# A hand-planned attention and feed-forward kernel: new keys for the planner's order on TensorE and in the head

## The chip, the cores and the metric

The kernel runs on one core of a Trainium2 chip. The core has five engines with an instruction stream each: TensorE (PE in the profile; its weight loads are listed as PEld), VectorE (DVE), ScalarE (ACT), GpSimd (POOL) and SyncE (SP), which here issues all the DMA transfers. The metric is the device time of one execution in microseconds, lower is better.

## The reference

Sparse attention over 8 batches, 8 heads, 576 positions and 64 dimensions, then a feed-forward network (FFN) on the 4608 tokens:

```python
scores = scale * np.matmul(q, k.transpose(0, 1, 3, 2))
thresh = np.max(scores, axis=-1, keepdims=True) - tau
scores = np.where(scores >= thresh, scores, -1000000000.0)
scores = scores - np.max(scores, axis=-1, keepdims=True)
attn = np.exp(scores)
attn = attn / (np.sum(attn, axis=-1, keepdims=True) + 1e-09)
out = np.matmul(attn, v)
...
h = x @ w_in
g = np.where(h >= beta, h, np.where(h <= -beta, 0.0, (h + beta) ** 2 / (4.0 * beta)))
return g @ w_out
```

Here x is the attention's output with the heads side by side (512 columns), w_in is 512 x 2048, w_out 2048 x 512, and beta is 1. The two weights come as 64-bit floats.

## The kernel before

**The planner.** The kernel doesn't write its instructions in program order. It describes each piece of work as an operation of a `Plan` (L40): an engine, an estimated cost, a key, what it comes after, and the buffers that it takes and uses. `Plan.order` (L73) then plays the engines forward in time: whenever an engine is free, it gets, among the operations whose predecessors are done and whose buffers are free, the one with the lowest key. The resulting list is the order in which the instructions are put into each engine's stream, and on the chip every engine works through its stream in that order. A key is thus a priority in the order, counted in units of attention tiles; an operation that isn't ready is passed over, whatever its key. Some chains have a fixed order of their own (`behind`): score products among themselves, products with V, first FFN products, second FFN products.

**Attention.** All matmuls work on values split into two 16-bit parts. Each batch has four pairs of heads. For each pair q and k are loaded, squared and summed for a scale, normalized on POOL, split by ACT and POOL, and copied by DMA into the layout that the matmuls need (`add_qk`, L287). V is handled once per batch (`add_v`, L369). The queries are cut into parts (batch, pair, half): the first half has 256 queries, the second 320, and all four first halves of a batch come ahead of the second halves. A part is cut into 4 or 5 tiles of 128 rows, 36 tiles in a batch, 288 in all. `add_tile` (L603) does one tile j, and nearly all its operations have the key j: the scores (PE, into one of two slots `s` of two PSUM banks each), the maximum (DVE), the exponential (ACT), the mask with the sum (DVE), the normalization (POOL), the split (ACT and POOL), and a transposing DMA into `eT`. When the last tile of a part is done, `add_av` (L669) multiplies by V on PE into one of three banks `ph` and splits the result into the buffer `x` of a group of tokens; its key is that of the part's last tile plus one. There are five `x` buffers, two of which serve as staging space for w_out until it is loaded.

**Weights.** `add_w` (L424) loads each weight in 16 units, converts each on DVE from 64 bits (three operations), sums its squares on PE (`gram`), and, when the scale is known, normalizes and splits it (ACT, ACT, POOL). The units of w_in are staged in eight places, those of w_out in two. The key of unit u comes from a function; its load stands 5 below it. For a pair of q and k the loads stand 6 below its key, for V 8 below.

**FFN.** A group of 256 tokens is worked on in pieces of 128 tokens, each in four steps of 512 hidden columns: `ffn1` (48 matmuls into a bank `ph`), `relu` and `square` (ACT), `gate` (DVE), `ghi` (ACT) and `glo` (DVE) into one of four buffers `g`, and `ffn2` (12 matmuls into the only bank `acc`); there are 144 such steps. The key `kf` of a step starts at the group's last attention tile plus `LEAD`, or goes on from the step before, and rises by 2 with each step, so that the four steps of 128 tokens take 8 units, as many as there are tiles for 128 tokens. After the fourth step `acc` is scaled by ACT and stored.

The loop that sets the keys of the loads:

```python
for b in range(B):
    for p in range(NPAIR):
        t0 = start[b, p, 0]
        add_qk(b, p, t0 if (b, p) != (0, 0) else -20)
    add_v(b, start[b, 0, 0] + (0 if b else 4))
add_w("i", lambda u: 0.7 * u - 2)
add_w("o", lambda u: 10 + 0.5 * u)
```

For batch 0 `start` is 0, 4, 8 and 12 for the four pairs.

Of the kernel before, what the change touches and what calls it, by code (L numbers as in the profile page):

```python
# [17 lines left out]
P = 128  # L18
GN = 256
FW = 512  # L20
LEAD = 8
EXPM = 0x7F000000
ESC = 2.0 ** 15

# [127 lines left out]
def attn_ffn_kernel(ctx: ExitStack, tc: tile.TileContext, qT, kT, vT, tau, w_in, w_out, out):  # L152
# [14 lines left out]
    NVB = NEB + 5  # L167
# [6 lines left out]
    plan = Plan()  # L174
# [53 lines left out]
    def ap(b, arr):  # L228
        return arr[b.slot]
# [40 lines left out]
    for i, (b, p, h) in enumerate(parts):  # L270
        first[i] = len(tiles)
        n, q0 = (S1, S0) if h else (S0, 0)
# [8 lines left out]
    start = {x: first[i] for i, x in enumerate(parts)}  # L281
# [267 lines left out]
    for b in range(B):  # L549
        for p in range(NPAIR):  # L550
            t0 = start[b, p, 0]
            add_qk(b, p, t0 if (b, p) != (0, 0) else -20)
        add_v(b, start[b, 0, 0] + (0 if b else 4))
    add_w("i", lambda u: 0.7 * u - 2)
    add_w("o", lambda u: 10 + 0.5 * u)

# [15 lines left out]
    for b in range(B):  # L574
        s, wi, wo = scs[:, b, :], wsc["i"], wsc["o"]
# [19 lines left out]
    part_tr = {}  # L595
    eTb = {}
    prev = {}

    def chained(name, o):
        prev[name] = o  # L600
        return o

    def add_tile(j):  # L603
        i, v, heads, col = tiles[j]
        b, p, h = parts[i]
        cb, qb, kb, ready, c2 = QK[b, p]
        s, e, x, m = plan.buf("s"), plan.buf("e"), plan.buf("hl"), plan.buf("sm")
        if i not in eTb:
            eTb[i] = plan.buf("eT")
            part_tr[i] = []  # L610

        def qk():
            q, k = ap(qb, qq), ap(kb, kk)
            for f in range(2):
                for l in range(2):
                    for hd, c in heads:
                        r = slice(0, P) if len(heads) == 1 else slice(hd * D, (hd + 1) * D)
                        n = r.stop - r.start
                        T.matmul(ap(s, s_ps)[r, f, :SH], q[:, hd, c : c + n], k[:, hd, l, f * SH : (f + 1) * SH], start=l == 0, stop=l == 1)  # L619

        def sv():
            return ap(s, s_ps)[:, :, :SH]

        def halves(t):
            return t.rearrange("p (f n) -> p f n", f=2)

        def smax():

            t, c = ap(m, sm), ap(cb, pc)
            V.tensor_reduce(t[:, 0:1], sv(), AX.XY, ALU.max, negate=True)  # L630
            V.tensor_scalar(t[:, 1:2], t[:, 0:1], c[:, 24 + v, 0:1], None, ALU.mult)  # L631
            V.tensor_scalar(t[:, 2:3], t[:, 0:1], -1.0, c[:, 27 + v, 0:1], ALU.mult, ALU.add)

        def sexp():
            A.activation(halves(ap(e, es)), sv(), AF.Exp, bias=ap(m, sm)[:, 1:2], scale=ap(cb, pc)[:, 24 + v, 0:1])  # L635

        def smask():
            t = ap(m, sm)
            V.scalar_tensor_tensor(halves(ap(e, es)), sv(), t[:, 2:3], halves(ap(e, es)), ALU.is_ge, ALU.mult, accum_out=t[:, 3:4])  # L639

        def sden():
            t = ap(m, sm)
            V.tensor_scalar(t[:, 4:5], t[:, 3:4], 1e-9, 1.0 / ESC, ALU.add, ALU.mult)  # L643
            V.reciprocal(t[:, 5:6], t[:, 4:5])

        def snorm():
            G.tensor_scalar(ap(e, es), ap(e, es), ap(m, sm)[:, 5:6], 1.0, ALU.mult, ALU.mult)  # L647

        def shi():
            A.activation(ap(x, hl)[:, :S], ap(e, es), AF.Copy)  # L650

        def slo():
            G.tensor_tensor(ap(x, hl)[:, S:], ap(e, es), ap(x, hl)[:, :S], ALU.subtract)  # L653

        def send():
            Y.dma_start_transpose(ap(eTb[i], eT)[:, :, col : col + P], ap(x, hl))

        o = chained("qk", plan.op("PE", 0.5 if len(heads) == 1 else 0.7, j, qk, ready, take=[s], uses=[qb, kb], behind=prev.get("qk")))
        o = chained("max", plan.op("DVE", 0.95, j, smax, [o, c2], take=[m], uses=[s, cb], behind=prev.get("max")))
        o = chained("exp", plan.op("ACT", 0.73, j, sexp, [o], take=[e], uses=[s, m, cb], behind=prev.get("exp")))  # L660
        o = plan.op("DVE", 0.82, j, smask, [o], uses=[s, m, e])
        o = plan.op("DVE", 0.26, j, sden, [o], uses=[m])
        o = chained("norm", plan.op("POOL", 0.77, j, snorm, [o], uses=[e, m], behind=prev.get("norm")))
        o = chained("hi", plan.op("ACT", 0.58, j, shi, [o], take=[x], uses=[e], behind=prev.get("hi")))
        o = plan.op("POOL", 1.26, j, slo, [o], uses=[e, x])
        o = chained("tr", plan.op("SP", 1.3, j, send, [o], take=[eTb[i]] if j == first[i] else [], uses=[x, eTb[i]], work=1.7, behind=prev.get("tr")))
        part_tr[i].append(o)

    def add_av(i):  # L669
        b, p, h = parts[i]  # L670
        n = S1 if h else S0
        pb = plan.buf("ph")
        vbuf, vready = VV[b, p]
        cuts, takes, xu = [], [], []
        p0 = h * S0
        for g, pieces in enumerate(groups):
            for gb_, t0, c0, m in pieces:
                lo, hi = max(t0, p0), min(t0 + m, p0 + n)
                if gb_ != b or lo >= hi:
                    continue  # L680
                if not xdone[g]:
                    takes.append(xbuf[g])
                xu.append(xbuf[g])
                cuts.append((g, slice(lo - p0, hi - p0), slice(c0 + lo - t0, c0 + hi - t0)))

        def av():
            o = ap(pb, ph)
            t = ap(eTb[i], eT)
            vt = ap(vbuf, vst)
            for k in range(NVB):  # L690
                kb = k if k < NEB else k - NEB
                for hd in range(2):
                    T.matmul(o[hd * D : (hd + 1) * D, :n], vt[:, k, hd * D : (hd + 1) * D], t[:, kb, hd * n : (hd + 1) * n],  # L693
                             start=k == 0, stop=k == NVB - 1)

        def xpart(g, l, c):
            return ap(xbuf[g], xb).bitcast(F16).rearrange("p (c l n) -> p c l n", c=NCC, l=2)[:, p, l, c]

        def hi():
            for g, src, c in cuts:  # L700
                A.activation(xpart(g, 0, c), ap(pb, ph)[:, src], AF.Copy, scale=1.0 / ESC)

        def lo():
            for g, src, c in cuts:
                V.scalar_tensor_tensor(xpart(g, 1, c), ap(pb, ph)[:, src], 1.0 / ESC, xpart(g, 0, c), ALU.mult, ALU.subtract)  # L705

        key = last[i] + 1
        m = len(cuts)
        o = chained("av", plan.op("PE", NVB * n / 2400 + 0.2, key, av, part_tr[i] + [vready], take=[pb], uses=[eTb[i], vbuf], behind=prev.get("av")))
        o = chained("avhi", plan.op("ACT", n / 1200 + 0.06 * m, key, hi, [o], take=takes, uses=[pb] + xu, behind=prev.get("avhi")))  # L710
        o = plan.op("DVE", n / 960 + 0.06 * m, key, lo, [o], uses=[pb] + xu)
        for g, _, _ in cuts:
            xdone[g].append(o)
            xlast[g] = max(xlast[g], last[i])

    for j in range(NS):
        add_tile(j)
        i = tiles[j][0]
# [7 lines left out]
    kf, nstep = 0.0, 0  # L726
    n, k = P, FW // P
    for g, c0 in [(g, c0) for g in range(NG) for c0 in range(0, gtok[g], P)]:
        kf = max(kf, xlast[g] + LEAD)
        ab = plan.buf("acc")  # L730
        ends = []
        bs = [b for b, _ in segs(g)]
        for fc in range(0, NFC, k):
            hb, tb, qb = plan.buf("ph"), plan.buf("asq"), plan.buf("g")
# [52 lines left out]
            wo = [wlo["o", x] for x in range(fc, fc + k)]  # L787
# [4 lines left out]
            o = chained("f1", plan.op("PE", 48 * 0.056, kf, ffn1, xdone[g] + wi, take=[hb], uses=[xbuf[g]], behind=prev.get("f1")))  # L792
            o = chained("relu", plan.op("ACT", 0.72 + 0.2 * (m - 1), kf, relu, [o] + fs, take=[tb], uses=[hb], behind=prev.get("relu")))
            o = plan.op("ACT", 0.52, kf, square, [o], uses=[tb])
            o = plan.op("DVE", 0.67 + 0.13 * (m - 1), kf, gate, [o], uses=[tb, hb])
            o = chained("ghi", plan.op("ACT", 0.57 + 0.15 * (m - 1), kf, ghi, [o], take=[qb], uses=[hb], behind=prev.get("ghi")))
            o = plan.op("DVE", 0.67 + 0.13 * (m - 1), kf, glo, [o], uses=[hb, qb])
            o = chained("f2", plan.op("PE", 12 * 0.216, kf + 1.0, ffn2, [o] + wo, take=[ab] if fc == 0 else [], uses=[qb, ab], behind=prev.get("f2")))
            ends.append(o)
            kf += 2.0  # L800

        mo = None
        if len(bs) > 1:
# [11 lines left out]
        o = plan.op("ACT", 0.57, kf, evict, [ends[-1], mo] + [oscale[b] for b in bs], take=[ob], uses=[ab])  # L815
# [41 lines left out]
```

## Time and profile before

| | |
|---|---|
| time, median of 3 runs | 1217.39 us (1214.46 to 1219.19) |
| the profiled execution | 1215.47 us, of which its span is 1213.2 |
| instructions | 31983 |
| mean granted clock of PE | 0.963 |
| bytes moved by DMA | 184.54 MB, mean 152 GB/s |

The profile is of one execution. Its span runs from the first to the last instruction of the core, and stage times are counted from its start. A row of the timeline gives start and duration in us, the engine, the line of the kernel, the operation, what it writes and reads, how many instructions the row merges and, in brackets, how long the engine was idle before and what ended the idle time. Matmuls are pipelined, so the distance between two starts tells more than a duration.

### The profile page before, as it was taken

How to read it: one execution, taken by the hardware profiler on the slowest of the kernel's cores; microseconds unless marked ns; L12 is line 12 of the kernel's file. 1: busy time of each engine (PE TensorE's matmuls, PEld its weight loads, DVE VectorE, ACT ScalarE, POOL GpSimd, SP SyncE). 2: the span in 40 equal slices, each digit the busy share in tenths (PEclk: the TensorE clock that was granted, in tenths of full speed). 3: DMA queues.
4: the chain of work that ended last, by engine and by line, in shares of the span. 5: the costliest groups of instructions: out<-in, count | busy, mean ns of one | idle time of the engine just before them, and what ended most of it. 6: DMA issues, size and time to landing. Idle time of an engine off the chain costs nothing.

```text
span 1213.2 us, 31983 instructions
## 1 busy us (share of the span) xinstructions
PE 1081.5 (89%) x11946; PEld 788.4 (65%) x11946; DVE 961.9 (79%) x2789; ACT 885.1 (73%) x1526; POOL 819.6 (68%) x939
## 2 busy tenths in 40 slices
PE   2334687999989999999999998999999999999998
PEld 1222564777667776776777776777667767777775
DVE  6978987779877897788877898888877997887422
ACT  6587688777777777787687777877777777776534
POOL 3688789657885688666985599766875689655200
PEclk9956798999989999999999999999999999999999
DMA  9999984946897579974997579955996589756200
GB/s 317 241 230 206 209 168 89 210 96 129 170 200 149 99 135 182 211 127 94 174 205 159 100 156 205 208 100 96 188 204 147 105 170 183 142 98 97 59 11 18
DMA packets 443818, 184.54 MB, mean 152 GB/s; under 512 B 406288, under 2 KB 414480, under 8 KB 443664
## 3 DMA queue, kind: packets, MB, share of 16 engines
q1 hardware_dynamic: 443664, 182.52, 74.7%
q8 instruction: 93, 1.52, 0.5%
q14 instruction: 61, 0.50, 0.1%
HBM read 45.09 MB, written 9.44 MB: 45 GB/s over the span
## 4 chain that ended last, share of the span: by engine, by line
PE 56%; DVE 19%; POOL 7%; ACT 7%; issue 5%; DMA 5%; SPq 1%; ACTq 0%; DVEq 0%; POOLq 0%
PE acc L781 22%; PE ph L754 21%; PE s L619 7%; PE ph L693 6%; DVE e L639 4%; DVE sm L630 4%; POOL hl L653 2%; POOL e L647 2%; DMA eT<-hl 2%; ACT e L635 1%; POOL nat L344 1%; DMA kk<-nat 1%; DVE ph L468 1%; DVE vb L409 1%; DVE ph L463 1%
## 5 line engine op out<-in xcount | busy, mean ns | idle before, releaser
L653 POOL TENSOR_TENSOR hl<-e,hl 128x576 f16<-128x576 f32 x288 | 368.0, 1283 | 98.8 <-ACT hl L650 96.4
L754 PE MATMUL ph<-x,WI 128*128 128x128 f16 x6912 | 409.3, 220 | 7.6 <-DVE x L705 4.6
L754 PEld LDWEIGHTS <-WI 128*128 128x128 f16 x6912 | 398.5, 98 | 22.1 <-issue 10.4
L781 PE MATMUL acc<-WO,g 128*128 128x512 f16 x1728 | 399.5, 382 | 4.6 <-DVE g L775 3.9
L647 POOL TENSOR_SCALAR e<-e,sm 128x576 f32<-128x576 f32 x288 | 218.7, 765 | 163.1 <-DVE sm L643 86.0
L781 PEld LDWEIGHTS <-g 128*128 128x128 f16 x1728 | 165.5, 98 | 195.3 <-DVE g L775 10.7
L635 ACT ACTIVATE e<-s,sm,pc 128x576 f32<-128x576 f32 x288 | 236.4, 828 | 69.7 <-DVE sm L631 56.9
L630 DVE TENSOR_REDUCE sm<-s 128x1 f32<-128x576 f32 x288 | 216.1, 751 | 65.5 <-PE s L619 62.3
L639 DVE SCALAR_TENSOR_TENSOR e<-s,sm,e 128x576 f32<-128x576 f32 x288 | 230.4, 813 | 30.4 <-ACT e L635 23.6
L650 ACT ACTIVATE hl<-e 128x576 f16<-128x576 f32 x288 | 194.7, 680 | 74.9 <-POOL e L647 68.6
L619 PE MATMUL s<-kk,qq 128*128 128x288 f16 (+1 forms) x1280 | 187.7, 298 | 51.2 <-DVE e L639 45.1
L619 PEld LDWEIGHTS <-qq 128*128 128x128 f16 (+1 forms) x1280 | 111.4, 103 | 103.2 <-issue 69.0
L767 DVE SCALAR_TENSOR_TENSOR ph<-ph,scs,asq 128x512 f32<-128x512 f32 (+1 forms) x160 | 111.6, 700 | 62.0 <-ACT asq L763 60.3
L760 ACT ACTIVATE asq<-ph,scs 128x512 f32<-128x512 f32 (+1 forms) x160 | 115.3, 731 | 51.5 <-PE ph L754 50.7
L693 PE MATMUL ph<-eT,vst 128*64 128x256 f16 (+1 forms) x1792 | 127.8, 295 | 8.2 <-DVE g L775 4.0
L775 DVE SCALAR_TENSOR_TENSOR g<-ph,scs,g 128x512 f16<-128x512 f32 (+1 forms) x160 | 109.0, 689 | 28.6 <-ACT g L771 28.2
L693 PEld LDWEIGHTS <-vst 128*64 128x64 f16 x1792 | 100.9, 113 | 32.5 <-issue 17.5
L771 ACT ACTIVATE g<-ph,scs 128x512 f16<-128x512 f32 (+1 forms) x160 | 100.8, 641 | 28.5 <-DVE ph L767 26.5
L763 ACT ACTIVATE asq<-asq 128x512 f32<-128x512 f32 x144 | 90.4, 628 | 1.7
L344 POOL TENSOR_TENSOR nat<-raw,nat 128x576 f16<-128x576 f32 x64 | 81.6, 1280 | 8.7 <-ACT nat L340 8.2
L631 DVE TENSOR_SCALAR sm<-sm,pc 128x1 f32<-128x1 f32 x288 | 61.7, 214 | 10.4
L340 ACT ACTIVATE nat<-raw 128x576 f16<-128x576 f32 x64 | 43.2, 679 | 34.5 <-POOL raw L337 27.2
(96 smaller groups left out, 779.4 us busy)
## 6 DMA issues: line engine op xcount, KB each, us to landing
kk<-nat SPq DMA_DIRECT2D x128, 144.0 KB, 3.1
raw<-in_q_dram SPq DMA_DIRECT2D x32, 288.0 KB, 3.8
raw<-in_k_dram SPq DMA_DIRECT2D x32, 288.0 KB, 3.9
raw<-in_v_dram SPq DMA_DIRECT2D x32, 288.0 KB, 3.7
qq<-nat SPq DMA_DIRECT2D x128, 72.0 KB, 2.3
WO<-in_moe_w_in_dram SPq DMA_DIRECT2D x16, 512.0 KB, 6.7
x<-in_moe_w_out_dram SPq DMA_DIRECT2D x16, 512.0 KB, 5.0
out_dram<-o SPq DMA_DIRECT2D x32, 256.0 KB, 3.0
```

The costliest lines, as they stand in the source:

```text
L619: T.matmul(ap(s, s_ps)[r, f, :SH], q[:, hd, c : c + n], k[:, hd, l, f * SH : (f + 1) * SH], start=l == 0, stop=l == 1)
L630: V.tensor_reduce(t[:, 0:1], sv(), AX.XY, ALU.max, negate=True)
L635: A.activation(halves(ap(e, es)), sv(), AF.Exp, bias=ap(m, sm)[:, 1:2], scale=ap(cb, pc)[:, 24 + v, 0:1])
L639: V.scalar_tensor_tensor(halves(ap(e, es)), sv(), t[:, 2:3], halves(ap(e, es)), ALU.is_ge, ALU.mult, accum_out=t[:, 3:4])
L647: G.tensor_scalar(ap(e, es), ap(e, es), ap(m, sm)[:, 5:6], 1.0, ALU.mult, ALU.mult)
L650: A.activation(ap(x, hl)[:, :S], ap(e, es), AF.Copy)
L653: G.tensor_tensor(ap(x, hl)[:, S:], ap(e, es), ap(x, hl)[:, :S], ALU.subtract)
L693: T.matmul(o[hd * D : (hd + 1) * D, :n], vt[:, k, hd * D : (hd + 1) * D], t[:, kb, hd * n : (hd + 1) * n], start=k == 0, stop=k == NVB - 1)
L754: T.matmul(h[:, i], WTh["i"][:, u, wl * 512 + c * P : wl * 512 + (c + 1) * P], x[:, cc, xl, c0 : c0 + P], start=m == 0, stop=m == 3 * NCC - 1)
L760: A.activation(tv()[:, :, c], hv()[:, :, c], AF.Relu, bias=scs[:, b, 2:3], scale=scs[:, b, 1:2])
L767: V.scalar_tensor_tensor(hv()[:, :, c], hv()[:, :, c], scs[:, b, 0:1], tv()[:, :, c], ALU.max, ALU.min)
L781: T.matmul(ap(ab, accs), gv()[:, i, gl], WTh["o"][:, fc + i, wl * 512 : (wl + 1) * 512], start=fc + i == 0 and m == 0, stop=fc + i == NFC ...
```

## The change

The constant `LEAD` goes from 8 to 12, and the keys get constants of their own:

- Score products on PE get the key j - 20 instead of j, products with V the last tile plus 1 - 6 instead of plus 1. The other operations of a tile keep their keys.
- `LEAD` moves all operations of an FFN step by 4. The second products get `kf + 8` instead of `kf + 1`. The rise of 2 for a step keeps its value under a name.
- In batch 0 the keys of the four pairs of q and k become -4.6, -1.7, 1.3 and 4.2 (they were -20, 4, 8 and 12), that of V 5.2 (it was 4). In later batches q and k come 4 earlier, V 2 later.
- Unit u of w_in gets -7.1 + 0.98 u (it was -2 + 0.7 u), unit u of w_out 1.9 + 0.68 u (it was 10 + 0.5 u).

```diff
-LEAD = 8
+
+KQ, KV = (-4.6, -1.7, 1.3, 4.2), 5.2
+KI, KO = (-7.1, 0.98), (1.9, 0.68)
+QN, VN = 4, -2
+QKP, AVP = 20, 6
+LEAD = 12
+KF, F2 = 2.0, 8
...
-            add_qk(b, p, t0 if (b, p) != (0, 0) else -20)
-        add_v(b, start[b, 0, 0] + (0 if b else 4))
-    add_w("i", lambda u: 0.7 * u - 2)
-    add_w("o", lambda u: 10 + 0.5 * u)
+            add_qk(b, p, t0 - QN if b else KQ[p])
+        add_v(b, start[b, 0, 0] - VN if b else KV)
+    add_w("i", lambda u: KI[0] + KI[1] * u)
+    add_w("o", lambda u: KO[0] + KO[1] * u)
...
-        o = chained("qk", plan.op("PE", 0.5 if len(heads) == 1 else 0.7, j, qk, ready, take=[s], uses=[qb, kb], behind=prev.get("qk")))
+        o = chained("qk", plan.op("PE", 0.5 if len(heads) == 1 else 0.7, j - QKP, qk, ready, take=[s], uses=[qb, kb], behind=prev.get("qk")))
...
-        o = chained("av", plan.op("PE", NVB * n / 2400 + 0.2, key, av, part_tr[i] + [vready], take=[pb], uses=[eTb[i], vbuf], behind=prev.get("av")))
+        o = chained("av", plan.op("PE", NVB * n / 2400 + 0.2, key - AVP, av, part_tr[i] + [vready], take=[pb], uses=[eTb[i], vbuf], behind=prev.get("av")))
...
-            o = chained("f2", plan.op("PE", 12 * 0.216, kf + 1.0, ffn2, [o] + wo, take=[ab] if fc == 0 else [], uses=[qb, ab], behind=prev.get("f2")))
+            o = chained("f2", plan.op("PE", 12 * 0.216, kf + F2, ffn2, [o] + wo, take=[ab] if fc == 0 else [], uses=[qb, ab], behind=prev.get("f2")))
...
-            kf += 2.0
+            kf += KF
```

## The prediction, made before the result was known

> **What bounds the kernel now.** I read the page first: how busy each engine is, then the chain that ended last.
>
> ```profile
> span 1213.2 us, 31983 instructions
> PE 1081.5 (89%) x11946; PEld 788.4 (65%) x11946; DVE 961.9 (79%) x2789; ACT 885.1 (73%) x1526; POOL 819.6 (68%) x939
> PE 56%; DVE 19%; POOL 7%; ACT 7%; issue 5%; DMA 5%; SPq 1%; ACTq 0%; DVEq 0%; POOLq 0%
> ```
>
> TensorE (PE) is busiest, and it holds 56% of the chain, DVE 19%. Busy time overstates pipelined matmuls, so I priced PE's four kinds of work from start to start in a full stretch of PE's timeline:
>
> ```profile
> 406.26 1.70 PE L693 MATMUL ph<-eT,vst 128*64 128x256 f16 x28
> 407.89 0.66 PE L619 MATMUL s<-kk,qq 128*128 128x288 f16 x4
> 408.39 2.75 PE L781 MATMUL acc<-WO,g 128*128 128x512 f16 x12
> 410.98 2.84 PE L754 MATMUL ph<-x,WI 128*128 128x128 f16 x48
> 413.66 1.14 PE L619 MATMUL s<-kk,qq 128*128 128x288 f16 x8
> ...
> 423.80 2.09 PE L693 MATMUL ph<-eT,vst 128*64 128x320 f16 x28
> 425.83 1.16 PE L619 MATMUL s<-kk,qq 128*128 128x288 f16 x8
> ```
>
> A product with V costs 1.63 us (256 queries) or 2.03 us (320), a tile's scores 0.50, a second FFN step 2.59, a first FFN step 2.68. The whole kernel has 32 and 32 products with V (117 us), 288 tiles of scores (144), 144 second steps (373) and 144 first steps (386): 1020 us. The span is 1213, so PE loses about 193 us. The table by stage says where:
>
> ```profile
> 0.00:150.00 150.00, 63.45 (x511) 43.66 (x512) 126.46 (x342) 100.89 (x180) 101.53 (x134) 0.77 1.00 243
> 150.00:220.00 70.00, 57.45 (x549) 38.75 (x548) 52.00 (x148) 56.99 (x102) 63.25 (x69) 0.93 0.68 135
> 220.00:1140.00 920.00, 892.20 (x10132) 657.13 (x10130) 762.66 (x2268) 697.41 (x1194) 654.80 (x738) 0.99 0.78 149
> 1140.00:1209.00 69.00, 68.41 (x763) 48.84 (x760) 20.78 (x36) 29.64 (x51) 0.00 (x0) 1.00 0.04 13
> ```
>
> Columns: stretch, its length, busy PE, weight loads, DVE, ACT, POOL, granted clock, DMA share, GB/s. **Head**, to 220: PE is busy 121 of 220 us, partly at a low clock; DMA is full until 150, then POOL is (63 of 70). **Middle**, to 1140: PE idles 27.8 us, and the clock of 0.99 on 920 us costs up to 9 more. **End**: PE is full, nothing to gain. The middle's idle time lies in patches:
>
> ```profile
> 320.00:400.00 80.00, 72.88 (x788) 51.81 (x786) 62.01 (x176) 59.02 (x103) 59.74 (x72) 0.96 0.87 175
> 400.00:440.00 40.00, 39.51 (x455) 29.52 (x453) 36.20 (x117) 30.77 (x55) 25.90 (x26) 1.00 0.55 101
> 440.00:520.00 80.00, 75.92 (x855) 55.18 (x854) 64.64 (x185) 61.30 (x112) 62.33 (x77) 1.00 1.00 186
> 720.00:780.00 60.00, 55.79 (x622) 39.84 (x621) 51.54 (x143) 48.29 (x87) 52.00 (x66) 1.00 0.98 205
> 980.00:1020.00 40.00, 36.92 (x413) 27.03 (x412) 33.38 (x103) 31.40 (x56) 36.20 (x49) 1.00 1.04 195
> 1020.00:1140.00 120.00, 120.00 (x1402) 90.11 (x1400) 94.34 (x273) 85.28 (x133) 73.33 (x77) 1.00 0.63 113
> ```
>
> They come once per batch, where q, k and v of the next batch are loaded and DMA is at 0.87 to 1.04; where DMA is at 0.55 or 0.63, PE is full. Inside the first patch:
>
> ```profile
> 335.53 2.08 PE L619 MATMUL s<-kk,qq 128*128 128x288 f16 x8 [4.16 <-DVE e L639]
> 337.40 1.06 PE L781 MATMUL acc<-WO,g 128*128 128x512 f16 x2
> 346.23 1.95 PE L754 MATMUL ph<-x,WI 128*128 128x128 f16 x32 [1.48 <-DVE x L705]
> ```
>
> PE waits 4.16 us for a mask and, later, 1.48 us for x, the attention's output. So the FFN has caught up with attention and has no work in store: whenever attention is late, PE stands still.
>
> **The change part by part.** No instruction is added or removed; only keys differ, so each edit costs or saves by order alone.
>
> *Attention leads (QKP 20, AVP 6, LEAD 8 to 12).* Before, a score product (key j) competes with FFN steps whose keys start 8 above the tile that completed x. When PE is the bound, the FFN wins until its key passes j, so attention is held back on PE to a lead of 8 tiles, of which its own pipeline (mask, transpose, product with V) uses most. After, PE always takes scores first, and DVE and ACT hold attention to a lead of 12. Four more tiles at 3.54 us of PE work per tile (1020 / 288) are a store of 14 us. The patches quoted lose 7.1, 4.1, 4.2 and 3.1 us each, all less than 14. So I take the middle's 27.8 us as covered, and part of the slow clock with it: 0.04 x 80 = 3.2 us in the stretch from 320, and 2 us for what else lies in the 0.99. Sum: **-33 us**, which is also the bound of what this edit can bring; nothing gained is the other.
>
> Can attention run faster than PE asks? POOL carries it:
>
> ```profile
> L653 POOL TENSOR_TENSOR hl<-e,hl 128x576 f16<-128x576 f32 x288 | 368.0, 1283 | 98.8 <-ACT hl L650 96.4
> L647 POOL TENSOR_SCALAR e<-e,sm 128x576 f32<-128x576 f32 x288 | 218.7, 765 | 163.1 <-DVE sm L643 86.0
> ```
>
> These two take 2.05 us a tile; all POOL work, 819.6 us over 288 tiles, is 2.85 us against PE's 3.54, so it can.
>
> *What the lead adds.* A score product issued early may find its slot of s (two of them) still read by the mask of the tile two before; behind it on PE wait all FFN steps and products with V, and behind these ACT and DVE's FFN work. The waits between 200 and 1100 (sum, times, longest):
>
> ```profile
> DVE sm L630 <- PE s L619: 52.2, 50, 3.8
> PE s L619 <- DVE e L639: 10.8, 13, 4.2
> PE ph L693 <- DVE g L775: 4.0, 4, 2.3
> ```
>
> At 50 tiles DVE had to wait for scores: there the product can move up at no cost to PE. At 13, PE waited, 0.83 us each. No row shows the new order, so: 0 at best; all 288 tiles x 0.83 = 239 us at worst. I take a value near the row: 20 more waits at scores (17 us) and four more at products with V (4 us): **+21 us**.
>
> The Trainium skill ("TensorE: Matmul & The Clock Gate", Part 3, The mechanism) says that matmuls start and end strictly in program order and that only weight loads are pulled ahead. By that rule a blocked score product holds ready FFN steps for its whole wait, which is the price used in the slow rival below. The trace doesn't contradict it, but shows no clear case: at 335.53 no FFN step was ready either.
>
> *Second FFN step last (F2 8 instead of 1).* It becomes PE's filler, up to the four buffers of g: 4 x 2.59 = 10.4 us in store. Danger: with g full, the step that fills g holds one of three banks ph, which products with V need too; that is the 4.0 us row, doubled above. KF is unchanged.
>
> *Head: weights and batch 0.* One weight load, from the page's list of transfers, and what ends the head, from the timeline:
>
> ```profile
> x<-in_moe_w_out_dram SPq DMA_DIRECT2D x16, 512.0 KB, 5.0
> ```
>
> ```profile
> 46.80 0.66 SPq L449 DMA_DIRECT2D x<-in_moe_w_out_dram  x1
> ...
> 132.54 2.84 PE L754 MATMUL ph<-x,WI 128*128 128x128 f16 x48 [1.71 <-DVE x L705]
> ...
> 143.97 0.59 SPq L449 DMA_DIRECT2D x<-in_moe_w_out_dram  x1
> ...
> 159.94 0.27 DVE L499 TENSOR_REDUCE ssq_o<-acc 128x1 f32<-128x128 f32 x1
> ...
> 166.22 2.28 POOL L528 TENSOR_TENSOR WO<-WO 128x512 f16<-128x512 f32 x2 [0.25 <-ACT WO L525]
> ...
> 177.41 2.75 PE L781 MATMUL acc<-WO,g 128*128 128x512 f16 x12
> ...
> 197.57 0.64 ACT L525 ACTIVATE WO<-WO 128x512 f16<-128x512 f32 x1
> ...
> 213.79 0.56 DVE L705 SCALAR_TENSOR_TENSOR x<-ph,x 128x256 f16<-128x256 f32 x2 [3.62 <-ACT x L701]
> 219.32 0.89 PE L754 MATMUL ph<-x,WI 128*128 128x128 f16 x13
> ```
>
> The 16 loads of w_out trickle through two staging buffers from 46.8 to 144 (6.5 us each); its scale is known at 160, and its splitting fills ACT and POOL until about 198, just when DMA has room and attention needs POOL. Batch 0 is complete only at 214, and the eight FFN steps of the first 256 tokens are used up by then: at 219 the FFN waits on attention with nothing left. The new keys put w_out at 1.9 to 12.1 instead of 10 to 17.5, so its loads, conversions and splits go ahead of transposes and tiles; w_in likewise starts at -7.1 instead of -2, and pairs 1 to 3 about 6 to 8 keys earlier. The price: the first pair's loads stand behind two w_in loads, 2 x 2.2 us (512 KB at the 243 GB/s of the first stage), and SP issues 32 weight loads ahead of transposes. While DMA is full, moving loads only exchanges what is late; the gain lies between 150 and 214, where splits (16 x 1.14 us on POOL, 18 us) move into the earlier stage, in which POOL has 48 us idle. Bounds: 64 us at POOL's 63/70 can shrink by 18, plus its own idle 6, so -24; or +4 from the late first pair. I take **-10**, since only about half of the splitting can start before 150. Here PE is idle anyway, so nothing else is late.
>
> *Later batches (QN 4, VN -2).* Their q and k load 4 tiles earlier and v 2 later, out of a ring of seven raw buffers: that spreads the 100% DMA patches, and its worth is in the -33.
>
> **Sum.** -33 + 21 - 10 = -22 us. The profiled execution took 1215.5 us (span 1213.2), 1.9 under the median of 1217.4. So 1193.5 on its scale, **1195** on the median's.
>
> **Rivals.** (a) *Attention runs ahead*, the forecast: 1178 to 1210, chance 0.55. (b) *The order hardly changes or the gain is spent*: the two s slots, not the keys, fix where scores go, or 43 us of gain meet 43 us of new waits (52 waits of 0.83). For it: 892 of 920 us busy leave little; the planner honours buffers before keys. Against: 50 waits of DVE on scores show that keys did delay them. 1217, within 6: chance 0.17. (c) *Slower: PE blocks at the front of its queue.* Scores now come at the first moment the planner thinks the mask is done; if DVE really runs later, the wait stands on the engine that is the bound. It decides where new waits x 0.83 pass the 43 us of gain: 52 waits, one tile in five or six. At 70 new waits, with the middle's gain and the head's half realised (22 us): +58 - 22 = 36, so 1253; at 43 waits 1231, the likeliest of this case. Chance 0.18. (d) *All of it works*: -33 - 24 = 57 with no new wait: 1160; chance 0.10.
>
> The Trainium skill's same page (Part 1) says that PE drops to half clock after an idle window of about 3.4 us. By it, waits of 0.83 us cost only themselves; longer ones, like the 4.16 us above (its stage shows 0.96), would cost more, and (c) would come out nearer 1253.
>
> **How the numbers follow.** A measurement of this kernel tells about 0.5% (6 us) from no change. Faster: (a) all but a sliver at 1211, and (d): 0.65. Same: 0.17. Slower: 0.18. The range leaves out the lower part of (d) and the upper part of (c): 1163 to 1230.
>
> **What would show it.** The last product with V before:
>
> ```profile
> 1140.38 2.09 PE L693 MATMUL ph<-eT,vst 128*64 128x320 f16 x28
> ```
>
> Right: in 220 to 1140 PE's idle falls under 15 us and the patches at DMA's peaks close; attention's last product with V moves from 1140 to well before 1120, and the pure FFN end grows while PE stays full; w_out's scale comes before 140 instead of 160, and batch 0 completes near 204 instead of 214. Wrong: scores waiting on masks far above 13 times and 10.8 us (case c); products with V waiting on DVE g; w_out still trickling until 140; batch 0 later than 214.

## The result and the profile after

The changed kernel takes 1179.03 us (median of 4 runs, 1176.29 to 1179.86), the kernel before, run beside it, 1215.93: a ratio of 0.969, with a 95% interval of 0.966 to 0.972. That is 37 us less, where 22 were forecast. The profiled execution took 1176.29 us, its span is 1174.5, 38.7 shorter. In the changed kernel's profile the lines have moved by 6: scores are L625, products with V L699, first FFN products L760, second ones L787, the mask L645.

The page of the changed kernel, in its lines for the span, the busy engines and the chain that ended last:

```profile
span 1174.5 us, 31921 instructions
PE 1072.8 (91%) x11946; PEld 780.8 (66%) x11946; DVE 966.4 (82%) x2789; ACT 883.2 (75%) x1526; POOL 817.2 (70%) x939
PE 56%; DVE 18%; POOL 9%; ACT 7%; issue 5%; DMA 4%; SPq 1%; ACTq 0%; POOLq 0%; DVEq 0%
```

The same work, and nearly the same shares: such lines say that something was won, not where. The table by stage does. Of the kernel before, the stretch from 220 to 1050 us (the changed kernel's attention ends soon after it):

```profile
220.00:1050.00 830.00, 802.20 (x9104) 590.48 (x9102) 694.61 (x2071) 635.16 (x1098) 606.60 (x690) 0.99 0.80 155
```

The changed kernel by stage:

```profile
0.00:150.00 150.00, 69.94 (x588) 48.13 (x589) 133.08 (x353) 104.58 (x186) 104.81 (x136) 0.86 0.99 242
150.00:220.00 70.00, 60.35 (x658) 43.55 (x656) 59.04 (x181) 63.70 (x115) 69.01 (x75) 1.00 0.76 145
220.00:1050.00 830.00, 822.60 (x9407) 604.63 (x9407) 737.53 (x2193) 662.93 (x1143) 638.09 (x725) 1.00 0.87 163
1050.00:1175.00 125.00, 119.89 (x1304) 84.52 (x1300) 36.72 (x65) 51.95 (x85) 5.29 (x5) 1.00 0.11 24
```

PE idles 7.4 us in the middle instead of 27.8, and its clock is 1.00 there. DVE, ACT and POOL do more in the same stretch (POOL 638 us instead of 607), so attention runs earlier. What PE has finished by 220 us is read from the groups of that stretch. Before:

```profile
L619 PE MATMUL s<-kk,qq 128*128 128x288 f16 (+1 forms) x184 | 36.2, 360 | 40.1 <-DVE e L639 34.3 <-DMA kk<-nat 5.7
L754 PE MATMUL ph<-x,WI 128*128 128x128 f16 x397 | 27.7, 237 | 4.9 <-DVE x L705 3.1 <-DVE g L775 1.7
L781 PE MATMUL acc<-WO,g 128*128 128x512 f16 x96 | 23.9, 406 | 0.2 <-ACT o L813 0.2
L693 PE MATMUL ph<-eT,vst 128*64 128x256 f16 (+1 forms) x224 | 19.3, 334 | 0.0
```

After:

```profile
L625 PE MATMUL s<-kk,qq 128*128 128x288 f16 (+1 forms) x208 | 41.0, 353 | 39.2 <-DVE e L645 35.3 <-DMA qq<-nat 2.5 <-DMA kk<-nat 1.1
L760 PE MATMUL ph<-x,WI 128*128 128x128 f16 x530 | 33.0, 224 | 1.9 <-DVE x L711 1.9
L699 PE MATMUL ph<-eT,vst 128*64 128x256 f16 (+1 forms) x252 | 22.5, 347 | 1.6 <-DVE g L781 1.5
L787 PE MATMUL acc<-WO,g 128*128 128x512 f16 x96 | 22.5, 379 | 2.2 <-ACT o L819 1.1 <-POOL WO L534 0.9 <-ACT WO L531 0.2
```

Priced with the prediction's full-clock prices (a kind's total over its number of matmuls), that is 78 us of work before and 90 after: the head gained **12 us**. The same count for 220 to 1050 gives 784 and 811: the middle gained **27 us**, 20.4 of it idle time; the rest, not taken apart further, lies in the clock (0.99 before, 1.00 now) and in gaps between matmuls. The two make about the 38.7 us.

What ends the head, from the changed kernel's timelines of PE, POOL and DVE (the sum for w_out's scale, the first two splits of w_out, the first second product, the completion of batch 0), and the last product with V:

```profile
145.68 0.17 PE L508 MATMUL ph<-ssq_o,ones 128*128 128x1 bf16 x1
...
151.56 2.28 POOL L534 TENSOR_TENSOR WO<-WO 128x512 f16<-128x512 f32 x2
...
160.85 1.46 PE L787 MATMUL acc<-WO,g 128*128 128x512 f16 x6
...
203.75 0.55 DVE L711 SCALAR_TENSOR_TENSOR x<-ph,x 128x256 f16<-128x256 f32 x2
...
1067.74 2.09 PE L699 MATMUL ph<-eT,vst 128*64 128x320 f16 x28
```

The sum for w_out's scale is formed at 145.7 instead of 161.3 us (the reduction ahead of it, which the prediction shows at 159.94, now starts at 142.1); second products begin at 160.9 instead of 177.4, batch 0 is complete at 203.8 instead of 213.8, and attention ends 73 us earlier. All waits of PE that the profile lists between 200 and 1100 us:

```profile
PE s L625 <- DVE e L645: 6.9, 15, 1.1
PE ph L760 <- DVE x L711: 0.3, 1, 0.3
```

Scores wait for masks about as often as before (15 times for 13) and for less, and the waits of products with V and of second products for g are gone.

### The profile page after: what moved, and what is told of

Its sections match the earlier page's. It is cut to its first block, busy times and chain, and to the rows that moved or that the text cites. A ratio compares the mean times of both kernels' runs of the same rounds, so it can differ in the third digit from the quotient of the medians.

```text
span 1174.5 us, 31921 instructions
## 1 busy us (share of the span) xinstructions
PE 1072.8 (91%) x11946; PEld 780.8 (66%) x11946; DVE 966.4 (82%) x2789; ACT 883.2 (75%) x1526; POOL 817.2 (70%) x939
## 4 chain that ended last, share of the span: by engine, by line
PE 56%; DVE 18%; POOL 9%; ACT 7%; issue 5%; DMA 4%; SPq 1%; ACTq 0%; POOLq 0%; DVEq 0%
PE ph L760 22%; PE acc L787 21%; PE s L625 7%; PE ph L699 6%; DVE e L645 3%; DVE sm L636 3%; POOL hl L659 3%; POOL e L653 2%; DVE vb L415 2%; POOL nat L350 2%; DVE ph L773 1%; ACT e L641 1%; DMA kk<-nat 1%; ACT hl L656 1%; DMA WO<-in_moe_w_in_dram 1%
## 5 line engine op out<-in xcount | busy, mean ns | idle before, releaser
L760 PE MATMUL ph<-x,WI 128*128 128x128 f16 x6912 | 410.7, 219 | 2.2 <-DVE x L711 2.2
L760 PEld LDWEIGHTS <-WI 128*128 128x128 f16 x6912 | 397.7, 98 | 21.9 <-issue 6.5
L787 PE MATMUL acc<-WO,g 128*128 128x512 f16 x1728 | 396.4, 379 | 2.2 <-ACT o L819 1.1
L653 POOL TENSOR_SCALAR e<-e,sm 128x576 f32<-128x576 f32 x288 | 222.0, 774 | 94.6 <-DVE sm L650 68.3
L787 PEld LDWEIGHTS <-g 128*128 128x128 f16 x1728 | 164.4, 98 | 179.5 <-issue 6.0
L645 DVE SCALAR_TENSOR_TENSOR e<-s,sm,e 128x576 f32<-128x576 f32 x288 | 231.5, 812 | 27.2 <-ACT e L641 22.4
L625 PE MATMUL s<-kk,qq 128*128 128x288 f16 (+1 forms) x1280 | 192.0, 298 | 46.3 <-DVE e L645 42.2
L625 PEld LDWEIGHTS <-qq 128*128 128x128 f16 (+1 forms) x1280 | 109.0, 103 | 104.2 <-issue 67.8
L699 PE MATMUL ph<-eT,vst 128*64 128x256 f16 (+1 forms) x1792 | 127.3, 296 | 1.6 <-DVE g L781 1.5
L781 DVE SCALAR_TENSOR_TENSOR g<-ph,scs,g 128x512 f16<-128x512 f32 (+1 forms) x160 | 109.0, 690 | 21.8 <-ACT g L777 21.4
L699 PEld LDWEIGHTS <-vst 128*64 128x64 f16 x1792 | 99.3, 113 | 26.2 <-issue 15.1
L769 ACT ACTIVATE asq<-asq 128x512 f32<-128x512 f32 x144 | 90.2, 627 | 2.1
L637 DVE TENSOR_SCALAR sm<-sm,pc 128x1 f32<-128x1 f32 x288 | 61.7, 214 | 10.4
L638 DVE TENSOR_SCALAR sm<-sm,pc 128x1 f32<-128x1 f32 x288 | 58.8, 204 | 0.0
```

The costliest lines, as they stand in the source:

```text
L760: T.matmul(h[:, i], WTh["i"][:, u, wl * 512 + c * P : wl * 512 + (c + 1) * P], x[:, cc, xl, c0 : c0 + P], start=m == 0, stop=m == 3 * NCC - 1)
L787: T.matmul(ap(ab, accs), gv()[:, i, gl], WTh["o"][:, fc + i, wl * 512 : (wl + 1) * 512], start=fc + i == 0 and m == 0, stop=fc + i == NFC ...
```

## The experiments

Each kernel is the one before or the changed one with some of the constants set differently; written in the new constants, the kernel before has QKP 0, AVP 0, F2 1, QN 0 and VN 0. The edits are shown in short, as changes of the constants and, in e11 and e12, of a number of buffers. A gain is the kernel's median against the median of the kernel before from the runs beside it; on this scale the whole change gains 36.9 us. Two columns were counted from the traces, with the prices used above: PE's work begun by 220 us and between 220 and 1050. The idle time is that of the table by stage from 220 to 1050. These three columns are of one execution each, which can lie some us off the median: the changed kernel's is 2.7 us below it, that of e8_lead20 2.7 above.

| kernel | median us | ratio to before (95%) | gain us | work by 220 | work 220 to 1050 | PE idle 220 to 1050 |
|---|---|---|---|---|---|---|
| before | 1215.9 | | | 78.2 | 783.7 | 27.8 |
| changed | 1179.0 | 0.969 (0.966 to 0.972) | 36.9 | 90.2 | 810.7 | 7.4 |
| e1_pe_keys | 1194.5 | 0.984 (0.982 to 0.986) | 19.9 | 81.0 | 802.7 | 13.4 |
| e2_head_keys | 1209.4 | 0.995 (0.993 to 0.997) | 5.0 | 86.2 | 781.6 | 29.4 |
| e3_next_batch | 1207.1 | 0.994 (0.992 to 0.996) | 7.3 | 80.0 | 790.2 | 24.6 |
| e4_no_score_lead | 1183.3 | 0.973 (0.971 to 0.976) | 31.1 | 88.2 | 805.7 | 13.5 |
| e5_lead_alone | 1216.9 | 0.999 (0.997 to 1.002) | -0.8 | 81.0 | 778.6 | 27.9 |
| e6_f2_alone | 1201.4 | 0.986 (0.983 to 0.989) | 14.6 | 77.1 | 797.1 | 18.1 |
| e7_lead8 | 1181.8 | 0.970 (0.968 to 0.973) | 34.2 | 89.5 | 806.2 | 10.6 |
| e8_lead20 | 1188.5 | 0.976 (0.974 to 0.978) | 27.5 | 81.3 | 804.8 | 12.1 |
| e9_attention_first | 1213.7 | 0.999 (0.998 to 1.001) | 1.3 | 77.4 | 787.1 | 27.0 |
| e10_f2_1 | 1187.9 | 0.978 (0.977 to 0.980) | 27.1 | 85.1 | 802.3 | 15.4 |
| e11_f2_two_g | 1209.4 | 0.995 (0.994 to 0.997) | 5.6 | 77.8 | 790.4 | 22.9 |
| e12_six_g | 1184.8 | 0.975 (0.972 to 0.977) | 30.2 | 85.8 | 807.4 | 8.7 |

### The three parts, each alone

**e1_pe_keys**, only the steady order changed:

```diff
+QN, VN = 0, 0
+QKP, AVP = 20, 6
+LEAD = 12
+KF, F2 = 2.0, 8
```

> Only the keys of the steady order (QKP 20, AVP 6, LEAD 12, F2 8); batch 0, weights and later batches as before. Theory A (attention's lead gives the FFN a store of work): PE's idle from 220 to 1100 us falls from 27.8 to under 12, and the time is 18 to 28 us below the kernel before, near 1192; batch 0 still completes near 214 us. Theory B (the patches close because the next batch is loaded earlier): no more than 8 us below, near 1210. Theory C (the head's weight keys bring most): no more than 8 us below.

19.9 us below, inside what theory A expected; the idle time fell to 13.4, not under 12. B and C, with at most 8 us for these keys, fall. One expectation missed: batch 0 was to complete near 214 us as before, and is complete at 204.3, as early as in the changed kernel, though with no new key for weights or batch 0's loads. DVE's row in e1, then in e2, the next kernel:

```profile
204.32 0.55 DVE L711 SCALAR_TENSOR_TENSOR x<-ph,x 128x256 f16<-128x256 f32 x2
...
210.78 0.55 DVE L711 SCALAR_TENSOR_TENSOR x<-ph,x 128x256 f16<-128x256 f32 x2
```

**e2_head_keys**, only batch 0 and the weights:

```diff
+KQ, KV = (-4.6, -1.7, 1.3, 4.2), 5.2
+KI, KO = (-7.1, 0.98), (1.9, 0.68)
```

> Only the keys of batch 0 and of the weights; steady order and later batches as before. Theory A: the head gains by itself, w_out's scale near 146 us instead of 160 and batch 0 complete near 202 us, 8 to 14 us below the kernel before, near 1205; idle in the middle stays above 22 us. Theory C: 25 us or more below. A rival to A (the head's gain needs attention to go first on PE): 0 to 5 us below.

5.0 us below, a miss on A's low side, with batch 0 complete at 210.8 where A had 202. By its size this is the rival's case (0 to 5), but not by its reason: the head does gain with no other key changed, 8.0 us of work by 220, and the sum for w_out's scale comes at 150.0 instead of 161.3 us, as the timeline of e2 shows:

```profile
149.96 0.17 PE L508 MATMUL ph<-ssq_o,ones 128*128 128x1 bf16 x1
```

But 2.1 us of it are given back before 1050 us: the middle's patches are about as they were (29.4 us of idle time).

**e3_next_batch**, only the loads of later batches:

```diff
+QN, VN = 4, -2
```

> Only QN 4 and VN -2: q and k of later batches 4 tiles earlier, v 2 tiles later. Theory A: within 5 us of the kernel before, patches of idle in the middle remain (above 20 us). Theory B: the patches close, 15 to 25 us below.

7.3 us below, more than A expected and far from B's 15. Idle time stays at 24.6 us; the new times of these loads help the middle by 6 us of work and don't close its patches. The three parts add up to 32.2 of 36.9 us, so they are nearly independent. e1's part is the largest, and the question is what in it.

### Inside the steady order: attention's lead or work in store

**e4_no_score_lead**, the changed kernel with

```diff
-QKP, AVP = 20, 6
+QKP, AVP = 0, 6
```

> The changed kernel with QKP 0: score products have the key j again, all else as changed. Theory A with the score key as its core: the FFN holds attention back on PE again; idle in the middle back to 15 us or more, 10 to 20 us above the changed kernel. Rival A2 (LEAD 12 and the late second products alone make the store of work): within 4 us of the changed kernel.

It loses 5.8 of the 36.9 us: less than A's 10 and a little more than A2's 4 (its interval just touches that of the changed kernel). The score key by itself is not the core. So LEAD and F2 were tried apart.

**e5_lead_alone**, the kernel before with

```diff
-LEAD = 8
+LEAD = 12
```

> The kernel before with LEAD 12 as its only change. Theory A (a larger lead of attention over the FFN is the store that closes the patches; four tiles are 14 us of work): 12 to 20 us below the kernel before, idle in the middle under 15 us. Theory D (the late second products are the store, as filler): within 5 us of the kernel before.

**e6_f2_alone**, the kernel before with

```diff
-KF, F2 = 2.0, 1.0
+KF, F2 = 2.0, 8
```

> The kernel before with F2 8 as its only change. Theory D: 12 to 20 us below the kernel before, idle in the middle under 15 us. Theory A: within 5 us of the kernel before, since the FFN still catches up with attention and the four buffers of g hold at most 10 us.

LEAD alone is worth nothing (-0.8 us, the interval holds 1); F2 alone is worth 14.6, though its idle time of 18.1 us is over the 15 expected. Theory A, with LEAD as the store, falls; D stands. The patch of the first batch shows how such a store is used. In the kernel before PE stood still for 4.16 us from 331 (the prediction's row at 335.53). In e6, on PE's timeline:

```profile
326.62 7.93 PE L787 MATMUL acc<-WO,g 128*128 128x512 f16 x36
334.38 1.14 PE L625 MATMUL s<-kk,qq 128*128 128x288 f16 x8
336.92 2.09 PE L699 MATMUL ph<-eT,vst 128*64 128x320 f16 x28 [1.39 <-DMA eT<-hl]
```

Three second products that lay ready, 36 matmuls in a row, fill part of the time in which the next tokens' x isn't there. Then the store is empty, and PE waits here too (1.39 us, then 3.23 us until 343.33). So this patch isn't closed by F2, nor is the second; the gain of e6 lies elsewhere: in the middle's other stretches its PE idles 6.6 us, against 16.6 before. The tables by stage, of e6 in the first two patches and of the changed kernel in the first:

```profile
320.00:400.00 80.00, 72.74 (x811) 55.11 (x808) 60.63 (x166) 60.12 (x110) 57.87 (x69) 0.96 0.91 182
440.00:520.00 80.00, 75.72 (x848) 54.76 (x846) 68.12 (x209) 65.47 (x118) 65.10 (x78) 1.00 1.00 197
...
320.00:400.00 80.00, 80.00 (x945) 60.01 (x945) 70.20 (x213) 67.13 (x118) 60.47 (x69) 1.00 0.91 166
```

Before, PE was busy 72.88 and 75.92 us there. In the changed kernel PE runs from 320 to 400 without a pause (in the 20 us ahead of it 1.1 are lost); a piece of it:

```profile
354.73 2.84 PE L760 MATMUL ph<-x,WI 128*128 128x128 f16 x48
357.41 0.65 PE L625 MATMUL s<-kk,qq 128*128 128x288 f16 x4
357.90 2.75 PE L787 MATMUL acc<-WO,g 128*128 128x512 f16 x12
360.49 2.84 PE L760 MATMUL ph<-x,WI 128*128 128x128 f16 x48
```

From the timelines of DVE and PE one can count, for each microsecond between 230 and 1050, how many steps have their g finished and their second product not yet begun: the store of ready work.

| kernel | mean store, steps | share of the time with none ready |
|---|---|---|
| before | 0.26 | 73% |
| e6_f2_alone | 1.76 | 12% |
| e11_f2_two_g | 1.03 | 18% |
| e10_f2_1 | 0.32 | 68% |
| changed | 2.18 | 1% |
| e12_six_g | 3.87 | 2% |

With F2 1 a second product has a lower key than the first product after it, so PE takes it as soon as it is ready, and when attention is late nothing is left. With F2 8 it yields to the first products of the next three steps, and up to four lie in g.

**e9_attention_first**, the kernel before with

```diff
-QKP, AVP = 0, 0
+QKP, AVP = 20, 6
```

> The kernel before with QKP 20 and AVP 6 as its only change: attention goes ahead of every FFN product on PE, second products stay next to first ones (F2 1). Theory E (late second products help because they let scores and products with V pass, so attention gets ahead): this does the same, 12 to 18 us below the kernel before. Theory D (late second products help as work in store in g that fills PE's gaps): within 5 us of the kernel before, idle in the middle above 22 us.

1.3 us below, the interval holds 1, idle time 27.0: letting attention pass is by itself worth nothing that can be told. Nor does it pass further in e6. Count, again for each microsecond from 230 to 1050, the attention tiles whose product with V is done, less two for each first FFN step begun (a step's share of tiles): this lead is 18.9 tiles before, 19.3 in e9 and 17.7 in e6. E falls here.

**e10_f2_1**, the changed kernel with

```diff
-KF, F2 = 2.0, 8
+KF, F2 = 2.0, 1.0
```

> The changed kernel with F2 1. Theory D: the store is gone, 12 to 20 us above the changed kernel, with PE waiting for g at second products again as before (3.9 us at 7 of them between 200 and 1100). Theory E: scores and products with V still lead, within 5 us of the changed kernel.

It loses 9.8 of the 36.9 us, just under D's 12 and well over E's 5. The store is gone (0.32), and PE waits for g at second products again:

```profile
PE acc L787 <- DVE g L781: 2.6, 5, 0.8
```

But the middle still does 802 us of work, 18.6 more than before, with no store of second products. So the other keys together do much of the work without it, and the first two patches, which F2 alone leaves open, are nearly closed. e10 by stage:

```profile
320.00:400.00 80.00, 78.20 (x873) 56.03 (x871) 68.56 (x201) 63.94 (x111) 61.29 (x72) 1.00 0.89 174
440.00:520.00 80.00, 80.00 (x931) 59.75 (x928) 69.66 (x199) 63.71 (x108) 58.03 (x61) 1.00 0.88 165
```

In the first patch PE idles, in one execution each, 1.8 us in e10 and 0.8 in e1, but 4.9 in e5, 6.8 in e9, 7.1 in e3 and 7.3 in e6. What e10 and e1 share is LEAD, QKP and AVP together. Attention's lead, counted as in e9, is 25.9 tiles in e10, against 21.8 in e1 and in e5, 20.3 in e3 and 19.3 in e9. If the parts add up here as well, LEAD, QKP and AVP are worth 27.1 - 5.0 - 7.3 = 14.8 us without F2, an estimate, where each part of them alone (e5, e9) gives nothing. That is as much as F2 alone, and the two together give 19.9 (e1): the two ways of having work in store, g for PE and x for the FFN, replace each other in part. LEAD, QKP and AVP without F2, QN and the head's keys were not run, so their share stays an estimate.

### How much store

**e11_f2_two_g**, e6 with half the room:

```diff
-    gb = ring("g", 4, [2 * FW], F16)
+    gb = ring("g", 2, [2 * FW], F16)
```

> e6_f2_alone with two buffers g instead of four: second products stay late in the order, but at most two finished steps can wait in store. Theory D (work in store in g): the gain of 14.6 us is gone, 10 us or more above e6 and within 6 us of the kernel before or above it; first products lead second ones by about 2 steps or less instead of 3.3. Theory F (the late key by itself orders PE's work better, whatever is in store): within 5 us of e6, near 1201.

It gains 5.6 us where e6 gained 14.6, with 1.03 steps in store instead of 1.76. Nine of the 14.6 us go with the room, nearly D's 10; the rest stays, and F's "near 1201" is refuted. The lead of first products begun over second products begun, 3.0 steps (3.2 in e6), was expected at 2 and hardly fell: of these steps 1.9 are not finished yet, against 1.4 in e6. A step that finds g full has to wait in its bank ph, so the count that matters is the one of finished steps.

**e7_lead8**, the changed kernel with

```diff
-LEAD = 12
+LEAD = 8
```

> The changed kernel with LEAD 8. Theory A: 10 to 16 us above the changed kernel, PE waits for x again and the idle in the middle is over 15 us. Theory D: within 4 us of the changed kernel.

2.7 us are lost, less than the intervals can tell apart; A expected 10 to 16. With F2 8 in place, LEAD hardly matters between 8 and 12.

**e8_lead20**, the changed kernel with

```diff
-LEAD = 12
+LEAD = 20
```

> The changed kernel with LEAD 20. Theory A: the patches are closed already (7.4 us of idle left in the middle, none of it on x), so the time stays within 4 us of the changed kernel. A rival (more lead is still worth time): 5 us or more below. Another (five x buffers fill, products with V hold banks of ph): 5 us or more above.

It loses 9.4 us, the size of the last rival. Its reason shows little in the waits: between 220 and 1100 us PE waits 0.5 us at products with V and 3.0 us at first FFN products (0.3 in the changed kernel). But the planner can also put a lack of banks into the order, where no wait shows it, so the rival isn't excluded. By 220 PE has done 81.3 us of work instead of 90.2, and 6 us less in the middle, though attention's lead there is 29.0 tiles (25.4 in the changed kernel): a longer lead isn't more time gained. In the head, where the FFN has nothing to spare, a larger LEAD may only put its steps behind attention's; this was not tested apart.

**e12_six_g**, the changed kernel with

```diff
-KF, F2 = 2.0, 8
+KF, F2 = 2.0, 12
...
-    gb = ring("g", 4, [2 * FW], F16)
+    gb = ring("g", 6, [2 * FW], F16)
```

> The changed kernel with six buffers g and F2 12: more room for the store. Theory D says that the store is large enough already: the middle has 7.4 us of idle left, 6.9 of it at scores that wait for masks, which more store can't cover, so within 4 us of the changed kernel. Rival (a larger store is still worth time): 5 us or more below, which would make it the best version.

It loses 6.7 us, a little outside the 4 that D allowed and opposite to its rival. The store grows to 3.87 steps, and the idle time doesn't fall (8.7 us): the room of four was enough. In the profiled executions 4 us are lost in the head's work by 220 and 3 in the middle; why is open. No kernel that was run is faster than the changed one.

## Why the prediction was right and where it was not

- *What bounds.* Right. PE's losses before were the head and the patches at the change of batches, and both shrank: 12 us of work more by 220, idle time in the middle from 27.8 to 7.4.
- *Attention leads, -33 us.* The size is about that of the middle's gain, 27 measured, but in part by luck: I gave all of it to QKP, AVP and LEAD, by an argument of four more tiles in store, and nothing to F2. LEAD alone gained nothing (e5), QKP and AVP alone nothing that can be told (e9), and LEAD 8 in the changed kernel costs 2.7 us (e7), so the four tiles aren't the store. The three together may well work as I had it: with them the first patch closes even without F2 (e10), and they are worth some 15 us by the estimate there.
- *Second FFN step last.* I called it PE's filler, up to 10.4 us in store, and gave it no term. Alone it is worth 14.6 us (e6), and taking it out costs 9.8 (e10). The row at 335.53 didn't lead there: neither a first nor a second product was ready, and I took this for a lack of x only. Second products can be kept for such a place, and before only 0.26 of them lay ready on average. In this very patch they don't suffice (e6 still loses 7.3 us in it); what F2 alone gains lies in the stretches outside the first two patches.
- *What the lead adds, +21 us.* This is the step that made the sum too small. I took 24 more waits. Measured are 15 waits at scores for 13, 6.9 us instead of 10.8, and none for 4 at products with V. An early score product rarely blocks PE: the planner puts it down only once its slot of s is free by its own clock, and the waits that remain are 1.1 us at most.
- *Head, -10 us.* Right in size: 12 us of work. e2 by itself shows 8 of these 12. The way was only half as forecast. The reduction for w_out's scale came at 142.1, not before 140, and its splits, which I wanted ahead of 150, started at 151.6 instead of 166.2. POOL is now full from 150 to 220 (69.0 of 70 us, where it had been 63.3). And batch 0, complete at 203.8 as forecast, owes this mainly to the steady order: 204.3 in e1, 210.8 in e2.
- *Later batches.* Forecast as part of the -33; e3 shows 7.3 us for it alone.
- *The rivals.* Case (b), that buffers and not keys set the order, falls. Case (c), PE blocked at the front of its queue, falls with the 6.9 us. Case (d), everything works with no new wait, gave 57 us, 24 of them in the head; with the head's -10 it would be 43, and the measured 37 lie between that and the forecast's 22. So the forecast's case holds, near its fast edge of 1178.

## What to carry to other kernels

Where one engine is the bound and its work comes in two stages, let the later stage yield to the earlier one and give it buffers to wait in: finished inputs are work in store for the moments in which the supply is late, and serving them at once keeps the store empty (0.26 steps before, 2.18 after). Count that store from the trace, as finished minus begun, before pricing an order; a lead that is written into keys isn't the lead that the engines have. When several keys move at once, try each alone and each taken out, and then the ones that did nothing alone together: here F2 was worth 14.6 us alone and 9.8 when taken out, while LEAD, and QKP with AVP, did nothing alone, and yet in the kernels that have them together the first patch closes, which F2 alone leaves open.
